# Seven products instead of eight for the experts' second product

## The chip, the cores and the metric

The kernel runs on one core of one Trainium2 chip. The metric is the device time of one execution in microseconds (us), as the median of the runs; the profile is of one further execution.

## The reference, cut to what matters

Attention (left out here) gives rows that a first MLP turns into `x`, 2304 tokens of 512 numbers. The part that the change touches is the last stage, eight experts that see every token; `P` is a 2304x8 table of weights, `F` is 1024:

```python
out = np.zeros((N, D), dtype=np.float32)
for e in range(E):                        # 8 experts
    h = np.maximum(x @ w1[e], 0.0)        # first product,  2304x512 @ 512x1024
    ye = h @ w2[e]                        # second product, 2304x1024 @ 1024x512
    out += P[:, e:e + 1] * ye
```

Everything is fp32. A number is held as a high and a low fp32r part, and one fp32 product is three matmuls: high by high, high by low, low by high (`mm3`, L79 to L82).

## The kernel before, in words

The expert stage starts some 655 us into the span and lasts to its end. It runs in *units* (L952 on). An expert's 1024 hidden columns are cut in two *blocks* (`NJ`), each of 256 columns from the lower and 256 from the upper half of `F` (`BF`), so there are 16 blocks. The 18 tiles of 128 tokens form three groups of six (`NUN`, `UP`), and a unit is one block for one group: 48 units.

In a unit, `hidden` (L882) makes the first product by Strassen's scheme in the variant with shared sums: seven products of halves in place of eight, in the order t1, b11, b22, t2, b21, t3, t4 of the operands made of x. Each product is done for two column tiles q = 0, 1 of 128 hidden columns: six matmuls that stream 384 tokens. A q step is called an *H step* here: 14 per unit, 84 matmuls of 128x384. The sums and differences of x are made once, kept in DRAM (`xs`), and loaded again for every unit through the ring `xr` of `XR` = 6 buffers (L737). The sums of w1 are made on POOL by `w1_prep` (L700) into the ring `w1o`. Products that are used more than once stay in PSUM and are accumulated on, or copied by ACT to a tile `u` (`kept`) and added by DVE (`plus`, L892). ReLU and the split into high and low parts is `relu_halves` (L875): ACT writes the high part (L877), DVE the low one (L878).

The second product is plain. Behind every second H step of a unit, `outputs` (L926) does one of the six token tiles of the unit before: four hidden tiles `h` by four tiles `w2o`, 12 matmuls of 128x512 into one PSUM bank `ps_acc`. That is called an *O step*, six per unit, 72 matmuls. DVE then scales the bank by a column of `pm` (that is `P`) and adds it to `acc` in SBUF (L944); in the first expert, where `pm` is not there yet, ACT copies (L938) or DVE adds (L940), and from the second expert on `acc` is scaled once on POOL (L943). The tiles `w2o` are made by `w2_prep` (L728): POOL writes the high part (`hi_pool`, L70) and the low part (`lo_pool`, L76) of each of four raw tiles of 128x512.

Each engine works through its instructions in one order, which a scheduler has fixed when the kernel is built; only waits on other engines move them. All loads go through one queue of SP, also in order: the loads of `xr`, and those of w1 and w2 (`w_load`, L680) into the ring `raw2`. A load whose buffer is not free holds back all loads behind it.

Of the kernel before, what the change touches and what calls it, by code (L numbers as in the profile page):

```python
# [21 lines left out]
def tile_kernel(ctx: ExitStack, tc, q, k, v, w_phi, w_in, w_out, w_gate, w1, w2, out):  # L22
# [37 lines left out]
    def bank(tag):  # L60
        return psp.tile([P, 512], F32, tag=tag, name="ps_" + tag, bufs=PS_BUFS[tag])
# [4 lines left out]
    def hi_act(dst, src, scale=1.0):  # L66
        nc.scalar.activation(dst, src, AF.Copy, scale=scale)
# [631 lines left out]


    def w1_prep(b):
        (a11, a12), (a21, a22) = (tuple(raw.pop((b, False, r, k)) for k in range(2)) for r in range(2))

        def add(x, y, op):
            t = wp.tile([P, 2, BF], F32, tag="ws", name="ws", bufs=3)
            nc.gpsimd.tensor_tensor(out=t, in0=x, in1=y, op=op)
            return t
# [12 lines left out]
        keep("s2", s2)  # L720
        yield
        keep("a12", a12)
        yield
        keep("s3", add(a11, a21, ALU.subtract))
        yield
        keep("a22", a22)
        yield

    def w2_prep(b):
        for i in range(2 * QB):  # L730
            w2t[b, i] = halves("w2o", 6, raw.pop((b, True) + divmod(i, QB)))
            yield

    def take(g, n):
        for _ in range(n):
            next(g, 0)
# [2 lines left out]
    WITH = {"t1": "s1", "b11": "a11", "b22": "s4", "t2": "s2", "b21": "a12", "t3": "s3", "t4": "a22"}  # L739
    units = [(b, c) for b in range(len(blocks)) for c in range(NUN)]  # L740
    wanted = [(c, o) for _, c in units for o in XOPS]
    XR = 6
    xring = []

    def x_ahead(n):
# [117 lines left out]
            )  # L863
            yield

    UB, HB = 8, 10

    side_work = []

# [5 lines left out]
    def relu_halves(src):  # L875
        t = hp_.tile([P, 2, UW], F32R, tag="h", name="h", bufs=HB)
        nc.scalar.activation(t[:, 0], src, AF.Relu)  # L877
        nc.vector.scalar_tensor_tensor(out=t[:, 1], in0=src, scalar=0.0, in1=f32(t[:, 0]), op0=ALU.max, op1=ALU.subtract)  # L878
        return t

    def hidden(b, c, n0, got):
        T, A, X = {}, {}, {}

        def kept(name, q, ps):
            T[name, q] = t = hp_.tile([P, UW], F32, tag="u", name="u", bufs=UB)
            nc.scalar.copy(t, ps)  # L888

        def plus(name, q, ps):  # L890
            t = T.pop((name, q))
            nc.vector.tensor_tensor(out=t, in0=ps, in1=t, op=ALU.add)  # L892
            return t

        for i, o in enumerate(XOPS):
            x_ahead(n0 + i + XR)
            x = xring[n0 + i]
            for q in range(QB):
                if o in ("t1", "b21"):
                    X[q] = bank("att")[:, 0:UW]  # L900
                if o == "b11":
                    A[q] = bank(("h", "kv")[q])[:, 0:UW]
                ps = (X if o in ("t1", "b22", "b21") else A)[q]
                product(ps, wops[b, WITH[o]], x, q, o in ("t1", "b11", "b21"))
                if b == 0 and q == 0:
                    for kh, t in {"t1": [(0, 1)], "b11": [(0, 0), (0, 1)], "b22": [(1, 1)], "b21": [(1, 0)]}.get(o, ()):
                        gate_add(x, kh, t)
                if o == "t1":
                    kept("p5", q, ps)
                elif o == "b11":  # L910
                    kept("p1", q, ps)
                elif o == "b22":
                    kept("p53", q, ps)
                elif o == "t2":
# [12 lines left out]

    def outputs(b, ti, hs, t):
        _, acc, pm = out_pool
        e, j = blocks[b]  # L930
        ps = bank("acc")
        ts_ = slice(t * P, (t + 1) * P)
        for i, h in enumerate(hs):
            w = w2t[b, i]
            mm3(ps, h[:, 0, ts_], h[:, 1, ts_], w[:, 0], w[:, 1], i == 0, i == 2 * QB - 1)
        a = acc[:, ti, :]
        if b == 0:
            nc.scalar.copy(a, ps)  # L938
# [12 lines left out]
    n0 = 0
    for b, c in units:  # L952
        got = {}
        for i, _ in enumerate(hidden(b, c, n0, got)):
            if not out_pool:
                with tc.high_priority(offset=-100):
                    make(2)
            if i % QB == QB - 1 and behind:
                outputs(*behind.pop(0))
        if not out_pool:  # L960
            make(99)
            ectx.close()
            mo = ctx.enter_context(tc.tile_pool(name="mo", bufs=1, reuse_waits="tile"))
            out_pool += [mo, mo.tile([P, NTT, DM], F32, name="acc"), mo.tile([P, NTT, E], F32, name="pm")]
            take(w2_prep(0), 9)
        n0 += len(XOPS)
        if b == 0:
            side_work.append(gate_end(c))
            next(side_work[-1])
            if c == NUN - 1:  # L970
                side_work.append(sinkhorn())
        behind = [
            (b, 2 * (UP * c + i) + t, [got["%d%d" % (r, t + 1), q] for r in (1, 2) for q in range(QB)], i)
            for t in (1, 0) for i in range(UP)
        ]
# [44 lines left out]
```

## Time and profile before

| | |
|---|---|
| median of 3 runs (lowest, highest) | 2190.03 us (2187.73, 2192.64) |
| the profiled execution's own time | 2189.35 us |
| its span | 2187.4 us |
| PE (matmul) busy | 2158.2 us, 99% |
| DVE, ACT, POOL busy | 48%, 32%, 23% |
| granted TensorE clock, mean of the span | 0.998 |

The profiled execution is 0.68 us under the median, and its span is 1.95 us shorter than its own time. A busy PE says only that matmuls follow each other without a gap; how close they follow is read from the starts of consecutive rows.

### The profile page before, as it was taken

How to read it: one execution, taken by the hardware profiler on the slowest of the kernel's cores; microseconds unless marked ns; L12 is line 12 of the kernel's file. 1: busy time of each engine (PE TensorE's matmuls, PEld its weight loads, DVE VectorE, ACT ScalarE, POOL GpSimd, SP SyncE). 2: the span in 40 equal slices, each digit the busy share in tenths (PEclk: the TensorE clock that was granted, in tenths of full speed). 3: DMA queues.
4: the chain of work that ended last, by engine and by line, in shares of the span. 5: the costliest groups of instructions: out<-in, count | busy, mean ns of one | idle time of the engine just before them, and what ended most of it. 6: DMA issues, size and time to landing. Idle time of an engine off the chain costs nothing.

```text
span 2187.4 us, 28996 instructions
## 1 busy us (share of the span) xinstructions
PE 2158.2 (99%) x11047; PEld 1903.2 (87%) x11047; DVE 1054.0 (48%) x1753; ACT 707.1 (32%) x1445; POOL 509.9 (23%) x537
## 2 busy tenths in 40 slices
PE   8999999999999999999999999999999999999999
PEld 6787888888888889998999899989998999899987
DVE  6998765754325264344334433443344334433443
ACT  6766655653223322222222222222222222222221
POOL 1001211100304133423313143131423313143100
PEclk9999999999999999999999999999999999999999
DMA  7798665647628555655555565655655556555553
GB/s 209 263 294 274 191 199 161 206 144 242 240 87 273 208 188 184 218 189 203 201 193 206 183 212 182 218 201 184 214 191 203 200 193 210 183 213 179 206 191 99
DMA packets 208699, 439.55 MB, mean 201 GB/s; under 512 B 74009, under 2 KB 130969, under 8 KB 208561
## 3 DMA queue, kind: packets, MB, share of 16 engines
q1 hardware_dynamic: 207280, 437.37, 59.3%
q8 instruction: 88, 1.44, 0.3%
q10 hardware_dynamic: 1280, 0.33, 0.1%
q14 instruction: 51, 0.41, 0.1%
HBM read 399.51 MB, written 38.12 MB: 200 GB/s over the span
## 4 chain that ended last, share of the span: by engine, by line
PE 93%; DVE 2%; ACT 2%; DMA 2%; SPq 1%; issue 1%; ACTq 0%; DVEq 0%
PE ps_acc L81 15%; PE ps_acc L82 15%; PE ps_acc L80 14%; PE ps_att L80 6%; PE ps_att L81 6%; PE ps_att L82 6%; PE ps_h L80 6%; PE ps_h L82 6%; PE ps_h L81 6%; PE ps_kv L82 4%; PE ps_kv L80 4%; PE ps_kv L81 4%; PE ps_att L86 1%; PE ps_kv L86 1%; DMA xs_t<-xo 1%
## 5 line engine op out<-in xcount | busy, mean ns | idle before, releaser
L944 DVE SCALAR_TENSOR_TENSOR acc<-ps_acc,pm,acc 128x512 f32<-128x512 f32 x252 | 189.1, 750 | 624.1 <-PE ps_acc L82 615.8
L82 PE MATMUL ps_acc<-w2o,h 128*128 128x512 f32 x1152 | 454.6, 395 | 0.0
L81 PE MATMUL ps_acc<-w2o,h 128*128 128x512 f32 x1152 | 453.9, 394 | 0.0
L80 PE MATMUL ps_acc<-w2o,h 128*128 128x512 f32 x1152 | 449.1, 390 | 0.3 <-ACT lt L855 0.3
L877 ACT ACTIVATE h<-u 128x384 fp32r<-128x384 f32 x288 | 140.6, 520 | 592.0 <-DVE u L892 592.0
L82 PEld LDWEIGHTS ps_acc<-w2o,h 128*128 128x128 f32 x1152 | 216.4, 188 | 45.9
L80 PEld LDWEIGHTS ps_acc<-w2o,h 128*128 128x128 f32 x1152 | 217.0, 188 | 39.8 <-ACT lt L855 0.7
L81 PEld LDWEIGHTS ps_acc<-w2o,h 128*128 128x128 f32 x1152 | 216.5, 188 | 39.9
L70 POOL TENSOR_SCALAR w2o<-raw 128x512 fp32r<-128x512 f32 x64 | 47.0, 735 | 649.4 <-PE ps_acc L82 557.4
L878 DVE SCALAR_TENSOR_TENSOR h<-u,h 128x384 fp32r<-128x384 f32 x288 | 190.6, 690 | 11.7
L80 PE MATMUL ps_att<-xr,w1o 128*128 128x384 f32 x576 | 194.0, 337 | 0.0
L82 PE MATMUL ps_att<-xr,w1o 128*128 128x384 f32 x576 | 193.8, 336 | 0.0
L81 PE MATMUL ps_att<-xr,w1o 128*128 128x384 f32 x576 | 193.3, 336 | 0.0
L888 ACT COPY u<-ps_att 128x384 f32<-128x384 f32 x192 | 92.1, 480 | 228.1 <-PE ps_att L82 228.1
L80 PE MATMUL ps_h<-xr,w1o 128*128 128x384 f32 x384 | 131.3, 342 | 0.0
L82 PE MATMUL ps_h<-xr,w1o 128*128 128x384 f32 x384 | 130.8, 341 | 0.0
L81 PE MATMUL ps_h<-xr,w1o 128*128 128x384 f32 x384 | 129.7, 338 | 0.0
L82 PE MATMUL ps_kv<-xr,w1o 128*128 128x384 f32 x384 | 128.4, 334 | 0.0
L80 PE MATMUL ps_kv<-xr,w1o 128*128 128x384 f32 x384 | 128.3, 334 | 0.0
L81 PE MATMUL ps_kv<-xr,w1o 128*128 128x384 f32 x384 | 128.3, 334 | 0.0
L70 POOL TENSOR_SCALAR w1o<-ws 128x512 fp32r<-128x512 f32 x64 | 40.7, 636 | 309.2 <-PE ps_att L82 307.8
L80 PEld LDWEIGHTS ps_att<-xr,w1o 128*128 128x128 f32 x576 | 108.2, 188 | 4.3 <-DVE xf L545 0.3
(250 smaller groups left out, 4074.3 us busy)
## 6 DMA issues: line engine op xcount, KB each, us to landing
xr<-xs_t SPq DMA_DIRECT2D x192, 768.0 KB
xr<-xs_b SPq DMA_DIRECT2D x144, 768.0 KB
w<-scratch SPq DMA_DIRECT2D x128, 512.0 KB
raw<-in_moe_w_dram SPq DMA_DIRECT2D x128, 256.0 KB
scratch<-cw SPq DMA_DIRECT2D x32, 512.0 KB
xs_t<-xo SPq DMA_DIRECT2D x36, 256.0 KB
raw<-in_moe_w_in_dram SPq DMA_DIRECT2D x16, 512.0 KB
raw<-in_moe_w_out_dram SPq DMA_DIRECT2D x16, 512.0 KB
```

What stands on the lines that cost most here:

```text
L70: nc.gpsimd.tensor_scalar(dst, src, 1.0, 1.0, op0=ALU.mult, op1=ALU.mult)
L80: nc.tensor.matmul(o, lhsT=wh, rhs=xh, start=start, stop=False, skip_group_check=chk)
L81: nc.tensor.matmul(o, lhsT=wh, rhs=xl, start=False, stop=False, skip_group_check=chk)
L82: nc.tensor.matmul(o, lhsT=wl, rhs=xh, start=False, stop=stop, skip_group_check=chk)
L86: nc.tensor.matmul(o, lhsT=w[0], rhs=x[0], start=start, stop=stop, skip_group_check=chk)
L877: nc.scalar.activation(t[:, 0], src, AF.Relu)
L878: nc.vector.scalar_tensor_tensor(out=t[:, 1], in0=src, scalar=0.0, in1=f32(t[:, 0]), op0=ALU.max, op1=ALU.subtract)
L888: nc.scalar.copy(t, ps)
L944: nc.vector.scalar_tensor_tensor(out=a, in0=ps, scalar=pm[:, ti, e:e + 1], in1=a, op0=ALU.mult, op1=ALU.add)
```

## The change

From the second expert on (block 2 of 16), the second product is done by the same scheme of seven products instead of eight half products. The first expert's two blocks stay as they were.

- `inner` (new) makes seven operands of the hidden tiles for each q: three (`a11`, `a22`, `a12`) are ReLU results, four (s1 to s4) are sums or differences of such, new operations of DVE. Five of the seven are split by `split`: ACT writes the high part, POOL the low part; `a22` and `a12` go through `relu_halves`.
- `w2_prep` makes seven split tiles of w2 for a block (three loaded quarters and four sums) instead of four; the four sums are new on POOL.
- `seconds` (new) does seven products, each for three pairs of token tiles and two q: 21 *S steps* of six matmuls of 128x256 per unit. Products accumulate on top of each other in chains in four fixed PSUM banks, and DVE reads the running sum after each product, scales it and adds it to a quarter of `acc` (L1059): 21 readings of 128x256 per unit.
- A unit's S steps run beside the H steps of the next unit, one behind each even and two behind each odd H step.
- Rings: `xr` 6 to 5, `raw2` 5 to 4, `w1o` 10 to 8, `w2o` 6 to 8, `u` 8 to 10, `h` 10 to 14. The w2 loads come in 128x2x256 pieces, and the preparation is called at other places.

```diff
+    WSB, W2B = 3, 8
...
-                t = wp.tile([P, 2 * BF], F32, tag="raw2", name="raw2", bufs=5)
+                t = wp.tile([P, 2 * BF], F32, tag="raw2", name="raw2", bufs=4)
...
+                if second and e:
+                    t = t.rearrange("p (q d) -> p q d", q=QB)
+                    nc.sync.dma_start(t, w2[e, f0:f0 + BF, k * HK:(k + 1) * HK].rearrange("(q p) d -> p q d", p=P))
...
+    def combine(x, y, op):
+        t = wp.tile([P, 2, BF], F32, tag="ws", name="ws", bufs=WSB)
+        nc.gpsimd.tensor_tensor(out=t, in0=x, in1=y, op=op)
+        return t
...
-            wops[b, o] = halves("w1o", 10, src)
+            wops[b, o] = halves("w1o", 8, src)
...
+        (b11, b12), (b21, b22) = (tuple(raw.pop((b, True, r, k)) for k in range(2)) for r in range(2))
+        keep("b11", b11)
+        yield
+        t1 = combine(b12, b11, ALU.subtract)
+        keep("t1", t1)
+        yield
+        t2 = combine(b22, t1, ALU.subtract)
+        keep("t2", t2)
+        yield
+        keep("t3", combine(b12, b22, ALU.subtract))
+        yield
+        keep("b22", b22)
+        yield
+        keep("t4", combine(b21, t2, ALU.subtract))
+        yield
+        keep("b21", b21)
+        yield
...
-    XR = 6
+    XR = 5
...
-    UB, HB = 8, 10
+    UB, HB = 10, 14
...
+    def split(t, src):
+        hi_act(t[:, 0], src)
+        lo_pool(t[:, 1], src, t[:, 0])
+        return t
...
+    def inner(b, o, q, T, got, ps, plus):
+        if o == "t2":
+            T["r21", q] = t = plus("p53", q, ps)
+            nc.scalar.activation(t, t, AF.Relu)
+        elif o == "b21":
+            T["r11", q] = t = plus("p1", q, ps)
+            nc.scalar.activation(t, t, AF.Relu)
+            got["a11", q] = split(new_h(), t)
+            s3 = new_u()
+            nc.vector.tensor_tensor(out=s3, in0=T["r21", q], in1=t, op=ALU.subtract)
+            got["s3", q] = split(new_h(), s3)
+        elif o == "t3":
+            t = plus("p5", q, ps)
+            s1 = T.pop(("r21", q))
+            nc.vector.scalar_tensor_tensor(out=s1, in0=t, scalar=0.0, in1=s1, op0=ALU.max, op1=ALU.add)
+            got["s1", q] = split(new_h(), s1)
+            s2 = T["s2", q] = T.pop(("r11", q))
+            nc.vector.tensor_tensor(out=s2, in0=s1, in1=s2, op=ALU.subtract)
+            got["s2", q] = split(new_h(), s2)
+            got["a22", q] = relu_halves(t)
+        elif o == "t4":
+            got["a12", q] = relu_halves(ps)
+            s4 = new_u()
+            nc.vector.scalar_tensor_tensor(
+                out=s4, in0=ps, scalar=0.0, in1=T.pop(("s2", q)), op0=ALU.max, op1=ALU.subtract
+            )
+            got["s4", q] = split(new_h(), s4)
...
+    SECOND = (
+        ("a11", "b11", "a", 0, 0), ("s1", "t1", "x", 1, 1), ("s2", "t2", "a", 0, 1), ("s3", "t3", "a", 1, 1),
+        ("s4", "b22", "x", 0, 1), ("a22", "t4", "a", 1, 0), ("a12", "b21", "y", 0, 0),
+    )
...
+    def seconds(b, c, got):
...
+        at_ = {
+            "a": [(b0, 0, 1), (b0, 1, 0), (b1, 0, 1)],
+            "x": [(b2, 0, 1), (b2, 1, 0), (b1, 1, 0)],
+            "y": [(b3, 0, 1), (b3, 1, 0), (b2, 0, 1)],
+        }
...
+                for q in range(QB):
+                    h = got[ho, q][:, :, i * P:(i + 1) * P]
+                    mm3(ps, h[:, 0], h[:, 1], w[:, 0, q], w[:, 1, q], first and q == 0, True, True)
+                due.append((i, ps))
+                if i == 0:
+                    yield
+                    continue
+                for i_, ps in due:
...
+                    nc.vector.scalar_tensor_tensor(
+                        out=a, in0=ps, scalar=pm[:, ti, e:e + 1], in1=a, op0=ALU.mult, op1=ALU.add
+                    )
...
+            if pending:
+                take(pending, 1 + odd)
+            elif odd and behind:
                 outputs(*behind.pop(0))
+            if odd and c == NUN - 1 and b + 1 < len(blocks):
+                take(coming, 1)
+            if odd and c == 0 and b:
+                take(late, 1)
...
-            take(coming, (1, 3, 9)[c])
-            if c == 1:
+            take(coming, (0, 1, 9)[c])
+            if c == NUN - 1:
                 w_load(b + 1, True)
-            take(late, (0, 0, 2)[c])
-    for x in behind:
-        outputs(*x)
+                late = w2_prep(b + 1)
+    for _ in pending:
+        pass
```

On DVE, this is the part of a unit from its product t3 on, in the kernel before (`ps_h` and `ps_kv` are the banks of q = 0 and 1, L892 is `plus`, L878 the low part, L944 the reading):

```order
L892 TENSOR_TENSOR u_14012<-ps_h_14039,u_14012 128x384
L892 TENSOR_TENSOR u_14021<-ps_kv_14048,u_14021 128x384
L878 SCALAR_TENSOR_TENSOR h_14180<-u_14012,h_14180 128x384
L878 SCALAR_TENSOR_TENSOR h_14190<-u_14021,h_14190 128x384
L878 SCALAR_TENSOR_TENSOR h_14193<-u_14046,h_14193 128x384
L878 SCALAR_TENSOR_TENSOR h_14196<-u_14055,h_14196 128x384
L944 SCALAR_TENSOR_TENSOR acc_7297<-ps_acc_14199,pm_7298,acc_7297 128x512
L878 SCALAR_TENSOR_TENSOR h_14221<-ps_h_14039,h_14221 128x384
```

The same part on DVE with the change (L959 is now `plus`, L936 and L939 make s1 and s2, L906 is the low part, L1059 the reading, L945 makes s4):

```order
L959 TENSOR_TENSOR u_12936<-ps_h_12973,u_12936 128x384
L936 SCALAR_TENSOR_TENSOR u_13025<-u_12936,u_13025 128x384
L939 TENSOR_TENSOR u_12980<-u_13025,u_12980 128x384
L959 TENSOR_TENSOR u_12951<-ps_kv_12988,u_12951 128x384
L936 SCALAR_TENSOR_TENSOR u_13039<-u_12951,u_13039 128x384
L906 SCALAR_TENSOR_TENSOR h_13182<-u_12936,h_13182 128x384
L939 TENSOR_TENSOR u_12995<-u_13039,u_12995 128x384
L1059 SCALAR_TENSOR_TENSOR acc_7295<-ps_acc_9060,pm_7296,acc_7295 128x256 x2
L1059 SCALAR_TENSOR_TENSOR acc_7295<-ps_acc_9061,pm_7296,acc_7295 128x256
L906 SCALAR_TENSOR_TENSOR h_13206<-u_12951,h_13206 128x384
L906 SCALAR_TENSOR_TENSOR h_13237<-ps_h_12973,h_13237 128x384
L945 SCALAR_TENSOR_TENSOR u_13240<-ps_h_12973,u_12980 128x384
```

Five operations with two inputs in SBUF (L936, L939, L906 from `u`) now stand ahead of the readings of banks 9060 and 9061, which the next unit's first product writes again.

On POOL, this is a stretch of the preparation in the kernel before, where a block's last w2 tiles are split and the next block's w1 sums begin (L706 makes a sum `ws`; `raw2` are loaded quarters):

```order
L70 TENSOR_SCALAR w2o_17224<-raw2_16742 128x512
L76 TENSOR_TENSOR w2o_17224<-raw2_16742,w2o_17224 128x512
L706 TENSOR_TENSOR ws_17235<-raw2_17231,raw2_17233 128x512
L70 TENSOR_SCALAR w1o_17237<-ws_17235 128x512
L70 TENSOR_SCALAR w1o_17470<-raw2_17227 128x512
L76 TENSOR_TENSOR w1o_17237<-ws_17235,w1o_17237 128x512
L76 TENSOR_TENSOR w1o_17470<-raw2_17227,w1o_17470 128x512
L706 TENSOR_TENSOR ws_17473<-ws_17235,raw2_17227 128x512
L70 TENSOR_SCALAR w2o_17732<-raw2_17483 128x512
```

The same place on POOL with the change, at the end of the first unit of a block (L707 makes the sums; `h` are low parts of the hidden operands, the last four of the ten of a unit among them):

```order
L70 TENSOR_SCALAR w2o_13280<-raw2_12923 128x512
L76 TENSOR_TENSOR h_13199<-u_13039,h_13199 128x384
L76 TENSOR_TENSOR w2o_13280<-raw2_12923,w2o_13280 128x512
L76 TENSOR_TENSOR h_13203<-u_12995,h_13203 128x384
L707 TENSOR_TENSOR ws_13618<-raw2_13287,raw2_13289 128x512
L76 TENSOR_TENSOR h_13242<-u_13240,h_13242 128x384
L70 TENSOR_SCALAR w1o_13620<-ws_13618 128x512
L707 TENSOR_TENSOR ws_13708<-ws_13618,raw2_13283 128x512
L76 TENSOR_TENSOR w1o_13620<-ws_13618,w1o_13620 128x512
L707 TENSOR_TENSOR ws_13710<-raw2_13285,ws_13708 128x512
L707 TENSOR_TENSOR ws_13856<-raw2_13283,raw2_13287 128x512
L76 TENSOR_TENSOR h_13262<-u_13260,h_13262 128x384
```

The hidden operands' low parts now queue among the weights' preparation: `h_13262`, the last s4, stands behind four sums that wait for the load of `raw2_13289`.

On SP's queue, the loads around the same place before (`xs_1_b21` is product b21's operand for the second token group):

```order
L749 DMA xr_14171<-xs_1_t2_130 128x1536
L749 DMA xr_14213<-xs_1_b21_131 128x1536
L691 DMA raw2_14245<-in_moe2_w1_dram 128x2x256
L688 DMA raw2_14495<-in_moe2_w2_dram 128x512
L749 DMA xr_14252<-xs_1_t3_132 128x1536
```

And with the change:

```order
L777 DMA xr_13229<-xs_1_t2_130 128x1536
L695 DMA raw2_13289<-in_moe2_w1_dram 128x2x256
L777 DMA xr_13291<-xs_1_b21_131 128x1536
L689 DMA raw2_13974<-in_moe2_w2_dram 128x2x256
L777 DMA xr_13332<-xs_1_t3_132 128x1536
```

The load of `raw2_13974` takes the buffer of `raw2_13287`, which POOL's last sum above reads, and the operand of t3 for the second unit stands right behind it.

## Rows read from the trace of the kernel before

**Rows 1.** The page, part 1: busy time, share and instructions of each engine

```profile
PE 2158.2 (99%) x11047; PEld 1903.2 (87%) x11047; DVE 1054.0 (48%) x1753; ACT 707.1 (32%) x1445; POOL 509.9 (23%) x537
```

**Rows 2.** Stretches of one unit each: busy of PE, PEld, DVE, ACT, POOL; clock; DMA

```profile
1500.97:1532.25 31.28, 31.28 (x158) 28.23 (x157) 11.95 (x20) 6.79 (x14) 0.00 (x0) 1.00 0.51 176
1532.25:1563.53 31.28, 31.28 (x158) 28.23 (x157) 13.45 (x20) 6.80 (x14) 18.91 (x18) 1.00 0.63 230
1563.53:1594.81 31.28, 31.28 (x158) 28.23 (x157) 12.83 (x20) 6.79 (x14) 7.84 (x8) 1.00 0.56 193
```

**Rows 3.** Timeline of DVE, readings of acc: start, length, instruction, idle before

```profile
1533.53 0.75 DVE L944 SCALAR_TENSOR_TENSOR acc<-ps_acc,pm,acc 128x512 f32<-128x512 f32 x1 [2.21 <-PE ps_acc L82]
...
1559.94 0.75 DVE L944 SCALAR_TENSOR_TENSOR acc<-ps_acc,pm,acc 128x512 f32<-128x512 f32 x1 [0.99 <-PE ps_acc L82]
...
1564.81 0.75 DVE L944 SCALAR_TENSOR_TENSOR acc<-ps_acc,pm,acc 128x512 f32<-128x512 f32 x1 [2.20 <-PE ps_acc L82]
```

**Rows 4.** Timeline of PE: first matmul of 12 H, of 12 O, and after

```profile
1509.02 0.33 PE L80 MATMUL ps_att<-xr,w1o 128*128 128x384 f32 x1
...
1511.10 0.39 PE L80 MATMUL ps_acc<-w2o,h 128*128 128x512 f32 x1
...
1513.86 0.33 PE L80 MATMUL ps_h<-xr,w1o 128*128 128x384 f32 x1
```

**Rows 5.** Timeline of PE and PEld, first MLP: 12 matmuls of 128x256, and after

```profile
641.95 0.28 PE L80 MATMUL ps_att<-gh,w 128*128 128x256 f32 x1
641.95 0.19 PEld L81 LDWEIGHTS ps_att<-gl,w 128*128 128x128 f32 x1
642.06 0.28 PE L81 MATMUL ps_att<-gl,w 128*128 128x256 f32 x1
...
643.38 0.40 PE L80 MATMUL ps_h<-xhi,w 128*128 128x512 f32 x1
```

**Rows 6.** Groups of DVE by shape: count, then busy us, mean ns, idle before

```profile
L892 DVE TENSOR_TENSOR u<-ps_h,u 128x384 f32<-128x384 f32 x96 | 53.5, 558 | 50.3 <-PE ps_h L82 50.3
...
L509 DVE SCALAR_TENSOR_TENSOR u<-t,ps_kv 128x256 f32<-128x256 f32 x16 | 6.7, 421 | 7.5 <-ACT t L507 7.5
```

**Rows 7.** Tile h, low parts from SBUF: shortest, median and longest, ns

```profile
L878 DVE SCALAR_TENSOR_TENSOR h<-u,h x288: 545/553/1642, 668.9 to 2163.3; 128x384 fp32r<-128x384 f32 x144
```

**Rows 8.** Timeline of DVE, two sets of four low parts

```profile
1504.83 2.17 DVE L878 SCALAR_TENSOR_TENSOR h<-u,h 128x384 fp32r<-128x384 f32 x4
...
1536.11 3.88 DVE L878 SCALAR_TENSOR_TENSOR h<-u,h 128x384 fp32r<-128x384 f32 x4
```

**Rows 9.** Timeline of POOL beside the second of these sets

```profile
1536.38 0.75 POOL L70 TENSOR_SCALAR w2o<-raw 128x512 fp32r<-128x512 f32 x1 [39.52 <-PE ps_acc L82]
1537.22 1.47 POOL L76 TENSOR_TENSOR w2o<-raw,w2o 128x512 fp32r<-128x512 f32 x1
```

**Rows 10.** Groups of ACT and POOL by shape

```profile
L877 ACT ACTIVATE h<-u 128x384 fp32r<-128x384 f32 x288 | 140.6, 520 | 592.0 <-DVE u L892 592.0
...
L76 POOL TENSOR_TENSOR w1o<-ws,w1o 128x512 fp32r<-128x512 f32 x64 | 82.6, 1291 | 2.5
...
L70 POOL TENSOR_SCALAR w1o<-ws 128x512 fp32r<-128x512 f32 x64 | 40.7, 636 | 309.2 <-PE ps_att L82 307.8
...
L76 POOL TENSOR_TENSOR vl<-vr,vh 128x320 fp32r<-128x320 f32 x16 | 14.9, 951 | 0.2
...
L76 POOL TENSOR_TENSOR wpl<-wpr,wph 128x256 fp32r<-128x256 f32 x1 | 0.7, 724 | 0.0
```

**Rows 11.** Timeline of SP and POOL: a load, and the sum that waits for it

```profile
1538.71 0.38 SPq L691 DMA_DIRECT2D raw<-in_moe_w_dram  x1
...
1541.47 1.29 POOL L706 TENSOR_TENSOR ws<-raw,raw 128x512 f32<-128x512 f32 x1 [0.33 <-DMA raw<-in_moe_w_dram]
```

**Rows 12.** The page, part 6: issues of the two kinds of load

```profile
xr<-xs_t SPq DMA_DIRECT2D x192, 768.0 KB
...
raw<-in_moe_w_dram SPq DMA_DIRECT2D x128, 256.0 KB
```

More of the change, by code (lines that the diff above doesn't have):

```diff
@@ L698, in halves @@
         return t
+    def combine(x, y, op):
+        t = wp.tile([P, 2, BF], F32, tag="ws", name="ws", bufs=WSB)
+        nc.gpsimd.tensor_tensor(out=t, in0=x, in1=y, op=op)
+        return t
     def w1_prep(b):
         (a11, a12), (a21, a22) = (tuple(raw.pop((b, False, r, k)) for k in range(2)) for r in range(2))
[L704 to L707, printed above, removed]
+        add = combine
         def keep(o, src):
-            wops[b, o] = halves("w1o", 10, src)
+            wops[b, o] = halves("w1o", 8, src)
         s1 = add(a21, a22, ALU.add)
@@ L729, in w2_prep, with keep @@
     def w2_prep(b):
-        for i in range(2 * QB):
-            w2t[b, i] = halves("w2o", 6, raw.pop((b, True) + divmod(i, QB)))
-            yield
+        def keep(o, src):
+            w2t[b, o] = halves("w2o", W2B, src)
+        if blocks[b][0] == 0:
+            for i in range(2 * QB):
+                keep(i, raw.pop((b, True) + divmod(i, QB)))
+                yield
+            return
+        (b11, b12), (b21, b22) = (tuple(raw.pop((b, True, r, k)) for k in range(2)) for r in range(2))
[15 more added lines that the diff above has]
+        yield
     def take(g, n):
@@ L879, in relu_halves, with new_h, new_u @@
         return t
+    def split(t, src):
+        hi_act(t[:, 0], src)
+        lo_pool(t[:, 1], src, t[:, 0])
+        return t
+    def new_h():
+        return hp_.tile([P, 2, UW], F32R, tag="h", name="h", bufs=HB)
+    def new_u():
+        return hp_.tile([P, UW], F32, tag="u", name="u", bufs=UB)
+    def inner(b, o, q, T, got, ps, plus):
[25 more added lines that the diff above has]
+            got["s4", q] = split(new_h(), s4)
     def hidden(b, c, n0, got):
@@ L913, in hidden @@
                     kept("p53", q, ps)
+                elif b >= NJ:
+                    inner(b, o, q, T, got, ps, plus)
                 elif o == "t2":
@@ L948, in outputs @@
             side_work.pop(0)
+    SECOND = (
+        ("a11", "b11", "a", 0, 0), ("s1", "t1", "x", 1, 1), ("s2", "t2", "a", 0, 1), ("s3", "t3", "a", 1, 1),
+        ("s4", "b22", "x", 0, 1), ("a22", "t4", "a", 1, 0), ("a12", "b21", "y", 0, 0),
+    )
+    banks = []
+    def seconds(b, c, got):
+        _, acc, pm = out_pool
+        e, j = blocks[b]
+        if not banks:
+            banks.extend(bank("acc") for _ in range(4))
+        b0, b1, b2, b3 = banks
+        at_ = {
[3 more added lines that the diff above has]
+        }
+        seen, scaled = set(), set()
+        for ho, wo, ch, t, n in SECOND:
+            w = w2t[b, wo]
+            due = []
+            for i in range(UP):
+                pb, half, first = at_[ch][i]
+                first = bool(first) and ch not in seen
+                ps = pb[:, half * HK:(half + 1) * HK]
+                for q in range(QB):
[3 more added lines that the diff above has]
+                if i == 0:
+                    yield
+                    continue
+                for i_, ps in due:
+                    ti = 2 * (UP * c + i_) + t
+                    if b == NJ and ti not in scaled:
+                        scaled.add(ti)
+                        nc.gpsimd.tensor_scalar(
+                            acc[:, ti, :], acc[:, ti, :], pm[:, ti, 0:1], 1.0, op0=ALU.mult, op1=ALU.mult
+                        )
+                    a = acc[:, ti, n * HK:(n + 1) * HK]
+                    nc.vector.scalar_tensor_tensor(
+                        out=a, in0=ps, scalar=pm[:, ti, e:e + 1], in1=a, op0=ALU.mult, op1=ALU.add
+                    )
+                    if b == len(blocks) - 1 and wo in ("b21", "t4"):
+                        store(ti)
+                due = []
+                yield
+            seen.add(ch)
     behind = []
+    pending = None
     n0 = 0
@@ L957, in tile_kernel @@
                     make(2)
-            if i % QB == QB - 1 and behind:
+            odd = i % QB
+            if pending:
+                take(pending, 1 + odd)
+            elif odd and behind:
                 outputs(*behind.pop(0))
+            if odd and c == NUN - 1 and b + 1 < len(blocks):
+                take(coming, 1)
+            if odd and c == 0 and b:
+                take(late, 1)
         if not out_pool:
@@ L971, in tile_kernel @@
                 side_work.append(sinkhorn())
[L972 to L975, printed above, removed]
+        if b >= NJ:
+            pending = seconds(b, c, got)
+        else:
+            behind = [
+                (b, 2 * (UP * c + i) + t, [got["%d%d" % (r, t + 1), q] for r in (1, 2) for q in range(QB)], i)
+                for t in (1, 0) for i in range(UP)
+            ]
         if c == 0:
```

4 lines of the change are left out of this document (2 added, 2 removed).

## The prediction, made before the changed kernel was run

> **What bounds the kernel now.** I read the page's shares first: PE is busy 99% of the span, no other engine over 48% [rows 1]. A busy PE can still be a waiting one, so the second view is the table of stretches. One unit is 31.28 us, the distance of the same reading in two units (1533.53 and 1564.81) [rows 3]; in three such stretches PE is busy for all 31.28, at the full clock (1.00, the 2.4 GHz level), DVE for 12 to 13.5, ACT for 6.8, POOL for 0 to 18.9 [rows 2]. The third view says what fills them. PE's timeline has 12 H matmuls from 1509.02 to 1511.10, 2.08 us, and 12 O matmuls from there to 1513.86, 2.76 us [rows 4]. Readings a pair of H steps and one O step apart lie 4.87 us apart (1559.94, 1564.81) [rows 3]: 2.08 + 2.76 + 0.03, so a switch from one kind to the other costs about 0.03. Seven H pairs, six O steps and six switches make 14.56 + 16.56 + 0.18 = 31.30, the unit as measured. Only fewer or shorter matmul slots shorten it.
>
> **Matmuls removed and added.** 42 units (14 blocks of three) change. Each loses 72 O matmuls, 16.56 us, and gets 126 of 128x256. The first MLP has just such a run, each with a weight load of its own: 12 from 641.95 to 643.38, 1.43 us or 0.119 each [rows 5]. So 126 x 0.119 = 15.02, a gain of 1.54 per unit and of 64.9 in 42. That the columns fall by an eighth (32256 for 36864) but the time only by 9% is the price of 54 more matmuls.
> The weight loads last 0.19 in the record, longer than the 0.119 slot, yet a load stands beside each matmul and the next starts on time [rows 5]: they are hidden.
> The Trainium skill ("TensorE: Matmul & The Clock Gate", The mechanism) says that a weight load overlaps matmuls in flight only when its row group differs; all loads here take the whole array, so by it every S slot would hold a load and a matmul. The trace disagrees, with 0.119 for both.
>
> **Switches.** H and S steps alternate 14 times a unit instead of six: eight more at 0.03 [rows 3] are 0.24, or 10 in all; the 256-wide run of the MLP shows none at its ends [rows 5]. Bounds 0 and 10; I take 5.
>
> **DVE.** Before, a unit has 20 operations. After it has six additions `plus` at 0.558 [rows 6], eight operations with two SBUF inputs (s1, s2, s3, the low part of a22, two q each), four on PSUM (low part of a12, s4) at 0.558, and 21 readings of 128x256; the nearest row of that width is 0.421 [rows 6]. The two-input price depends on POOL: four low parts take 2.17 with POOL idle, 0.54 each, and 3.88 while POOL works, 0.97 each [rows 8, 9]; the longest of all is 1.64 [rows 7]. Sum: 3.35 + 4.3 to 7.8 + 2.2 + 8.8 = 18.7 to 22.2 of 29.8. That fits, so throughput is no bound; the place to look at is the end of a unit. From the end of t3's first H step (five pairs of 4.25 and one H step into the unit, 22.3; 0.2 for the drain of the last matmul, whose record, 0.33, outlasts its slot) two `plus`, five two-input operations and two readings stand before PE may write the same bank in the next unit's second slot, at 29.8 + 1.05 = 30.8. At 0.97 they need 1.12 + 4.85 + 0.84 = 6.8 and end at 29.3: 1.5 us to spare. I price it at nothing; above 1.27 per operation PE waits.
>
> **ACT** gets 16 operations of 0.52 for six [rows 10], so 6.8 + 5.2 = 12.0 of 29.8 [rows 2]; DVE's slack above is also that of what it feeds.
>
> **POOL.** A block has 14 split tiles (0.64 + 1.29) and eight sums (1.29) [rows 10], 37.3, plus 30 low parts of 128x384. No row has that width; 256, 320 and 512 took 0.72, 0.95 and 1.29 [rows 10], so 0.95 to 1.29, and I take 1.0, near the line through them: 30. Together 67 of a block's 89, up to 76 at the upper bound, 27 before [rows 2]. The tight place is the end of a block's first unit. The split of t4's tile can start at 21.4, when PE has left its buffer; three tile halves, five low parts and b21's last half later (2.6 + 5.0 + 1.3) it is 30.3. Then SP may load `raw2_13289`; a load of its size landed 2.7 us after its issue (1538.71 to 1541.44) [rows 11], so the next sum starts at 33.0, and with it seven operations (four sums, one split, one low part: 5.2 + 1.9 + 1.0) end at 41.1. Only then does SP issue `raw2_13974` and behind it t3's operand for the next unit. That is 768 KB, the load ahead 256 [rows 12]; at 345 GB/s (193 GB/s at a share of 0.56 [rows 2]) the 768 KB beyond the first 256 take 2.3 more, and the issue ahead 0.4 [rows 11], so it is there at 41.1 + 0.4 + 2.7 + 2.3 = 46.5, and wanted at 29.8 + 21.2 = 51.0. The last low part of s4 is done at 42.1 and wanted at 29.8 + 17.0 + 1.05 = 47.9. So 4.5 and 5.8 us to spare. Interference stretches POOL too: its operations beside the contended set took 0.75 and 1.47 for 0.64 and 1.29 [rows 9], some 0.15 each, 2.5 on this chain. It still holds, priced at nothing. The smaller `xr` ring costs only lead: four pairs, 17 us.
>
> **Small waits.** All these margins are of 1.5 to 6 us and 21 readings release banks in each unit; PE will not be as gapless as before. Between nothing and 1 us per unit I take 0.2: 8.
>
> **Sum.** The profiled execution took 2189.35: minus 64.9, plus 5, plus 8, is 2137.5; the median was 0.7 above it: 2138.
>
> **The rivals.**
> *POOL's chain is late.* Where the walk above is over 4.5 us longer, t3's operand comes late once a block, in 14 blocks. At 1.29 per low part (1.7 more for six), 0.4 of interference on some 16 operations (6.4) it is 8.1 longer, 3.6 late: 2138 + 14 x 3.6 = 2188; halfway, 2163. For it: POOL goes from 29% to 75% busy [rows 2] and holds SP's queue; against it: a quarter of the block is still free.
> *DVE is late in every unit (slower).* With POOL in work nearly all the time, a two-input operation waits out a POOL operation and more. If the five ahead of the readings take the longest seen, 1.64 [rows 7], they end at 32.7, 1.9 late, 80 us in 42 units: 2218. It decides from 1.27; at 1.56 each, the gain of 61 us is used up. For it: 0.97 and 1.64 come from a kernel with POOL at 29%. Against it: POOL is idle for long in a block's second unit, and 0.97 already is a stretch of full work.
> The Trainium skill ("SBUF — State Buffer", Who interferes with whom) says that a DVE instruction with two SBUF inputs contends with a GpSimd instruction that reads SBUF, an exclusive lock for the whole instruction; the 0.54 against 0.97 agree with it.
> *Small waits everywhere.* Where 21 readings and smaller rings cost the 1 us per unit of the bound above: 2130 + 42 = 2172.
> *Loads are not hidden at 256 columns (slower).* Were the 54 more loads paid at their recorded 0.19, a unit would be 10.3 longer instead of 1.5 shorter, over 2560. Rows 5 speak against it.
>
> **How the numbers follow.** PE stays the bound with small waits: 0.64, 2125 to 2158, 2138 the likeliest. POOL late or small waits everywhere: 0.19, 2158 to 2192. DVE late: 0.15, above 2185. Loads: 0.02. The range leaves out the fast end below 2122 and most of the slow cases: 2122 to 2188. A measurement of this kernel can tell about 0.2% (4 us) from no change. Faster: 0.64, most of the second case and the edge of the third, 0.81; same 0.05; slower 0.14.
>
> **What would show it.** In a stretch of one unit: its length 29.8 to 30.2 instead of 31.28; 12 S matmuls in 1.43; PE waits on DVE under 0.5 a unit; readings near 0.42; low parts of 384 on POOL near 1.0; two-input operations of DVE under 1.27 on average. Wrong it is if units come out over 31, and then PE's waits name the case: on DVE at the banks `ps_acc` early in a unit, on the load `xr` of t3 in a block's second unit, or none at all and slots longer than 0.119.

## The result, and the profile after

The changed kernel took 2133.73 us (median of 4 runs, 2127.82 to 2135.14), the kernel before 2191.33 beside it (4 runs, 2187.73 to 2192.64): a ratio of 0.9735, 95% interval 0.9712 to 0.9757. The forecast was 2138. The profiled execution is the fastest of the four, 2127.82 with a span of 2126.0. Its span is 61.4 us shorter than that of the profile before (2187.4), 3.8 more than the medians show.

Where the time went is read in five steps. The first is the page's part 1, after:

```profile
PE 2089.0 (98%) x13315; PEld 1956.8 (92%) x13315; DVE 1424.6 (67%) x2551; ACT 905.6 (43%) x1865; POOL 1134.7 (53%) x1097
```

Against [rows 1], PE has 2268 instructions more and 69 us less; it is still the bound. DVE, ACT and POOL together have some 1200 us more work.

Second, three stretches of 29.82 us of the kernel after, which answer to [rows 2] (columns as there):

```profile
1500.00:1529.82 29.82, 29.82 (x214) 29.75 (x214) 21.83 (x39) 11.48 (x24) 24.37 (x22) 1.00 0.51 191
1529.82:1559.64 29.82, 29.82 (x215) 29.82 (x214) 21.56 (x41) 11.72 (x25) 20.39 (x20) 1.00 0.65 226
1559.64:1589.46 29.82, 29.49 (x209) 29.20 (x208) 21.70 (x40) 11.40 (x25) 26.70 (x26) 1.00 0.60 212
```

The length of a stretch comes from an operation that occurs once a unit, s4 of q = 0. This is its group in the view of the tile `u`: count, shortest, median and longest in ns, first and last start:

```profile
L945 DVE SCALAR_TENSOR_TENSOR u<-ps_h,u x42: 537/541/543, 880.4 to 2103.1; 128x384 f32<-128x384 f32 x42
```

(2103.1 − 880.4) / 41 = 29.82 a unit, for 31.28 before. The three stretches give POOL 71.5 us of a block's 89.5, DVE 21.7 and ACT 11.5 a unit. In the third PE lacks 0.33.

Third, PE's timeline, the first slots of a unit:

```profile
1505.26 0.34 PE L80 MATMUL ps_att<-xr,w1o 128*128 128x384 f32 x1
...
1507.04 0.34 PE L80 MATMUL ps_att<-xr,w1o 128*128 128x384 f32 x1
...
1508.09 0.28 PE L80 MATMUL ps_acc<-w2o,h 128*128 128x256 f32 x1
...
1509.51 0.34 PE L80 MATMUL ps_h<-xr,w1o 128*128 128x384 f32 x1
...
1534.87 0.34 PE L80 MATMUL ps_att<-xr,w1o 128*128 128x384 f32 x1
```

An H step takes 1.05 (1507.04 to 1508.09), the 12 S matmuls behind it 1.42, this pair 4.25 (1505.26 to 1509.51), this unit 29.61, so a pair 4.23 on average. The next unit, up to the H step at 1564.46 below, takes 29.59. The prediction's slots alone, 14.56 and 15.02, make 29.58: a change of kind costs nothing that can be seen here. Before, it cost 0.03 [rows 3], and one row more of that trace shows where:

```profile
1515.97 0.39 PE L80 MATMUL ps_acc<-w2o,h 128*128 128x512 f32 x1
```

The H pair at 1509.02 in [rows 4], a unit's first, follows another H pair and takes 2.08. The pair at 1513.86 follows an O step and takes 2.11, up to this row. The starts in [rows 4] span both changes of kind and add up to 4.84, so the 0.03 lies inside the pair behind an O step.

Fourth, PE's waits over the whole span (us, times, longest), the largest group:

```profile
PE ps_acc L80 <- DVE acc L1059: 6.7, 17, 1.1
```

Of the 17, 14 stand at one place per block, the first S step of a block's first unit (4.8 us); three, 1.9 us with the longest, come after the last H step. PE's timeline at that place:

```profile
1564.46 0.34 PE L80 MATMUL ps_att<-xr,w1o 128*128 128x384 f32 x1
...
1566.00 0.36 PE L80 MATMUL ps_acc<-w2o,h 128*128 128x256 f32 x1 [0.33 <-DVE acc L1059]
...
1594.64 0.34 PE L80 MATMUL ps_att<-xr,w1o 128*128 128x384 f32 x1
```

The H step that begins at 1564.46 should hand over at 1565.51; the S step starts at 1566.00, 0.49 late, and this unit is 30.18 long. What it waited for is in DVE's timeline:

```profile
1558.07 1.26 DVE L936 SCALAR_TENSOR_TENSOR u<-u 128x384 f32<-128x384 f32 x1
1559.43 1.47 DVE L939 TENSOR_TENSOR u<-u 128x384 f32<-128x384 f32 x1
1560.83 0.54 DVE L959 TENSOR_TENSOR u<-ps_kv,u 128x384 f32<-128x384 f32 x1
1561.41 0.80 DVE L936 SCALAR_TENSOR_TENSOR u<-u 128x384 f32<-128x384 f32 x1
1562.13 1.65 DVE L906 SCALAR_TENSOR_TENSOR h<-u,h 128x384 fp32r<-128x384 f32 x1
1563.70 1.37 DVE L939 TENSOR_TENSOR u<-u 128x384 f32<-128x384 f32 x1
1564.99 1.26 DVE L1059 SCALAR_TENSOR_TENSOR acc<-ps_acc,pm,acc 128x256 f32<-128x256 f32 x3
```

and in POOL's beside it:

```profile
1558.88 1.61 POOL L707 TENSOR_TENSOR ws<-raw,ws 128x512 f32<-128x512 f32 x1
1560.45 1.34 POOL L76 TENSOR_TENSOR h<-u,h 128x384 fp32r<-128x384 f32 x1
1561.76 1.61 POOL L707 TENSOR_TENSOR ws<-raw,raw 128x512 f32<-128x512 f32 x1
1563.32 1.34 POOL L76 TENSOR_TENSOR h<-u,h 128x384 fp32r<-128x384 f32 x1
```

The five two-input operations ahead of the readings take 1.26 + 1.47 + 0.80 + 1.65 + 1.37 = 6.55, 1.31 each. POOL has no gap there, and its operations are stretched too: 1.61 for 1.30, 1.34 for 1.02. At the ends of the two units before, the same five took 5.59 (from 1499.27, also beside a POOL without gaps) and 5.26 (from 1528.89, POOL at work for three quarters of the time), 1.12 and 1.05 each, and the S step was not late.

Fifth, the end of the span: the first matmul behind the last H step, before and after, and PE's waits from there on in the kernel after:

```profile
2165.90 0.39 PE L80 MATMUL ps_acc<-w2o,h 128*128 128x512 f32 x1
```

```profile
2099.36 0.28 PE L80 MATMUL ps_acc<-w2o,h 128*128 128x256 f32 x1
PE ps_acc L80 <- DVE acc L1059: 1.9, 3, 1.1
```

From there to the end of the span it is 21.5 us before and 26.7 after, although the slots are as long: six O steps (16.56) have become the last two S steps of one unit and the 21 of the last (16.4 in all). These S steps have no H steps beside them. Up to the last matmul it is 3.0 us more, 1.9 of them in those waits, and behind it 2.2 more.

### The profile page after: what moved, and what is told of

It reads as the page before. It is cut to its first block, busy times and chain, and to the rows that moved or that the text cites. A ratio compares the mean times of both kernels' runs of the same rounds, so it can differ in the third digit from the quotient of the medians.

```text
span 2126.0 us, 35902 instructions
## 1 busy us (share of the span) xinstructions
PE 2089.0 (98%) x13315; PEld 1956.8 (92%) x13315; DVE 1424.6 (67%) x2551; ACT 905.6 (43%) x1865; POOL 1134.7 (53%) x1097
## 4 chain that ended last, share of the span: by engine, by line
PE 80%; DVE 9%; DMA 3%; issue 3%; ACT 2%; POOL 1%; SPq 1%; ACTq 0%; DVEq 0%; POOLq 0%
PE ps_acc L80 12%; PE ps_acc L82 12%; PE ps_acc L81 12%; PE ps_att L80 6%; PE ps_att L81 6%; PE ps_att L82 5%; PE ps_h L80 5%; PE ps_h L82 5%; PE ps_h L81 5%; PE ps_kv L81 3%; PE ps_kv L80 3%; PE ps_kv L82 3%; DVE u L939 2%; DVE acc L1059 2%; DVE u L936 1%
## 5 line engine op out<-in xcount | busy, mean ns | idle before, releaser
L80 PE MATMUL ps_acc<-w2o,h 128*128 128x256 f32 (+1 forms) x1908 | 552.8, 290 | 6.7 <-DVE acc L1059 6.7
L82 PE MATMUL ps_acc<-w2o,h 128*128 128x256 f32 (+1 forms) x1908 | 553.7, 290 | 0.0
L81 PE MATMUL ps_acc<-w2o,h 128*128 128x256 f32 (+1 forms) x1908 | 552.7, 290 | 0.0
L76 POOL TENSOR_TENSOR h<-u,h 128x384 fp32r<-128x384 f32 x420 | 465.0, 1125 | 159.6 <-ACT h L67 115.4
L1059 DVE SCALAR_TENSOR_TENSOR acc<-ps_acc,pm,acc 128x256 f32<-128x256 f32 x882 | 374.1, 473 | 212.1 <-PE ps_acc L82 208.1
L80 PEld LDWEIGHTS ps_acc<-w2o,h 128*128 128x128 f32 x1908 | 359.5, 188 | 17.4 <-ACT h L67 9.5
L67 ACT ACTIVATE h<-u 128x384 fp32r<-128x384 f32 x420 | 220.9, 526 | 344.4 <-DVE u L945 99.8
L82 PEld LDWEIGHTS ps_acc<-w2o,h 128*128 128x128 f32 x1908 | 360.9, 189 | 5.8
L81 PEld LDWEIGHTS ps_acc<-w2o,h 128*128 128x128 f32 x1908 | 360.4, 189 | 5.0
L707 POOL TENSOR_TENSOR ws<-raw,raw 128x512 f32<-128x512 f32 x60 | 82.6, 1377 | 136.7 <-DVE u L509 79.6
L70 POOL TENSOR_SCALAR E<-E 128x1024 fp32r<-128x1024 f32 (+1 forms) x24 | 22.4, 932 | 189.5 <-ACT E L305 107.9
L906 DVE SCALAR_TENSOR_TENSOR h<-u,h 128x384 fp32r<-128x384 f32 x120 | 122.0, 1025 | 1.1
```

Of the source, the lines that this page charges most:

```text
L70: nc.gpsimd.tensor_scalar(dst, src, 1.0, 1.0, op0=ALU.mult, op1=ALU.mult)
```

## The experiments

All ran beside the kernel before (2189.2 to 2190.5); ratios are to it. Units are measured as above.

**after_again: the changed kernel once more,** on the chip of actlow, early and threes.

> The changed kernel once more, as the measure for the others of this call. All theories: 2134 us, within 4. In its trace a block should again show one wait of PE on DVE of about 0.5 us, at the second slot of a block's first unit, and none elsewhere.

2134.28 (0.9742, 0.9728 to 0.9755), unit 29.82, PE's wait on DVE 6.7 us in 17 times again. Where this run differs from the first profile is ahead of the changed units: the first H step of all starts at 659.5 instead of 655.4, the first one with S steps beside it at 886.4 instead of 878.4, and the spans are 7.8 apart. So the spread between these two executions does not come from the changed units.

**actlow: POOL freed of the hidden operands' low parts.** ACT writes the high part a second time in their place; the subtraction is left out.

```diff
     def split(t, src):
         hi_act(t[:, 0], src)
-        lo_pool(t[:, 1], src, t[:, 0])
+        hi_act(t[:, 1], src)
```

> The ten low parts per unit that POOL makes for the hidden operands are written by ACT instead, as a second copy of the high part (the low part's subtraction is left out); POOL keeps only the weights. Theory (POOL's reads stretch DVE's operations with two SBUF inputs, and these cause the wait): the two-input operations fall from about 1.0 to 1.4 us to 0.55 to 0.8, the wait once a block is gone, 8 us less, about 2126. Rival (the operations are long by themselves, or ACT, from 12 to 17 us a unit, now becomes late): two-input operations over 1.0 still, or waits of PE on ACT, and 2134 or more.

2123.51 (0.9691, 0.9677 to 0.9705). No wait on DVE, POOL or ACT is left in the units; two stretches of it, columns as above:

```profile
1500.00:1529.50 29.50, 29.50 (x211) 29.50 (x211) 19.62 (x41) 15.43 (x36) 9.82 (x9) 1.00 0.58 207
1529.50:1559.00 29.50, 29.50 (x212) 29.50 (x211) 18.12 (x37) 14.10 (x32) 15.51 (x15) 1.00 0.58 199
```

PE is full. The stretches are 29.50 long after the mean distance of s4's starts, 29.51, which is short of a unit: the first two of the 42 starts lie only 26.6 apart. PE's own rows, the first matmul of two units, give 29.59, as in the third unit of a block with the change:

```profile
1502.76 0.34 PE L80 MATMUL ps_att<-xr,w1o 128*128 128x384 f32 x1
...
1532.35 0.34 PE L80 MATMUL ps_att<-xr,w1o 128*128 128x384 f32 x1
```

So 29.59 is what the slots need. And DVE's two-input operations got shorter, though nothing in them changed. Their groups (shortest, median, longest), first of the kernel after, then of this one:

```profile
L906 DVE SCALAR_TENSOR_TENSOR h<-u,h x120: 541/1022/1650, 668.1 to 2101.7; 128x384 fp32r<-128x384 f32 x120
L936 DVE SCALAR_TENSOR_TENSOR u<-u x84: 557/962/1362, 873.3 to 2097.0; 128x384 f32<-128x384 f32 x84
L939 DVE TENSOR_TENSOR u<-u x84: 557/1369/1471, 874.8 to 2099.2; 128x384 f32<-128x384 f32 x84
```

```profile
L906 DVE SCALAR_TENSOR_TENSOR h<-u,h x120: 539/555/1652, 669.2 to 2092.8; 128x384 fp32r<-128x384 f32 x120
L936 DVE SCALAR_TENSOR_TENSOR u<-u x84: 557/559/966, 876.3 to 2089.6; 128x384 f32<-128x384 f32 x84
L939 DVE TENSOR_TENSOR u<-u x84: 547/560/1544, 877.3 to 2090.5; 128x384 f32<-128x384 f32 x84
```

What POOL's low parts cost through the others is 11 us (2134.28 against 2123.51); by the units, (29.82 − 29.59) x 42 = 10.

**early: all readings earlier in DVE's order.**

```diff
+                    with tc.high_priority(offset=100):
                         nc.vector.scalar_tensor_tensor(
                             out=a, in0=ps, scalar=pm[:, ti, e:e + 1], in1=a, op0=ALU.mult, op1=ALU.add
                         )
```

> The readings of the sums get a higher priority, so that on DVE the three readings of a22's product stand ahead of s2 of q = 1 and of the low parts of a22, not behind. Theory (PE's only regular wait is the bank that those readings release, 0.5 to 0.6 us once in each of 14 blocks, because five two-input operations stand ahead of them): the wait goes and nothing else changes, 8 us less than the changed kernel, about 2126. Rival (DVE as a whole is late there, so the wait only moves to the next thing that DVE owes, a22's low part or the banks of the hidden products): 2134.

2157.31 (0.9848, 0.9834 to 0.9862), 23 us slower than the change. PE's largest wait, DVE's timeline, and the matmul that waits:

```profile
PE ps_h L80 <- DVE u L946: 18.9, 27, 1.8
```

```profile
1613.87 1.47 DVE L907 SCALAR_TENSOR_TENSOR h<-u,h 128x384 fp32r<-128x384 f32 x1 [1.07 <-ACT h L906]
1615.26 0.54 DVE L907 SCALAR_TENSOR_TENSOR h<-ps_h,h 128x384 fp32r<-128x384 f32 x1
1615.73 1.25 DVE L1061 SCALAR_TENSOR_TENSOR acc<-ps_acc,pm,acc 128x256 f32<-128x256 f32 x3
1616.90 0.54 DVE L946 SCALAR_TENSOR_TENSOR u<-ps_h,u 128x384 f32<-128x384 f32 x1
```

```profile
1617.50 0.44 PE L80 MATMUL ps_h<-xr,w1o 128*128 128x384 f32 x1 [0.97 <-DVE u L946]
```

Three readings now stand ahead of s4, which frees the bank `ps_h`, and DVE idles 1.07 with nothing to fill it. The stall of the S step is gone; a larger one stands at `ps_h`. Neither branch of the expectation had a loss.

**early2: only a22's readings earlier** (`offset=100 if ho == "a22" else 0` in the same place).

> Only the readings of a22's product are put forward on DVE; those of the last product y stay behind s4, whose operation releases the bank of the hidden product b11. The run with all readings forward was 23 us slower, with PE waiting 0.7 us in two of three units for s4 (L946), and its trace had DVE idle 1.07 us before the second low part of a22, which waits for ACT there. Theory (DVE's chain at a unit's end is tight, and its order decides which bank comes late; the slots of PE are the same): the wait for a22's readings goes, s4 is 0.9 us earlier than with all readings forward and comes just in time, a unit of 29.5 to 29.7 instead of 29.82, so 2122 to 2130. Rival (the idle gap before a22's second low part, now uncovered, makes s4 late in most units): units of 29.9 to 30.2, 2138 to 2150.

2133.09 (0.9739, 0.9726 to 0.9753), unit (2107.7 − 887.6) / 41 = 29.76. No wait of a block's first S step on DVE is left, but the unit still takes 29.98 (1510.81 to 1540.79), with smaller latenesses in place of that wait. No difference from the change that can be measured: less than the theory expected, and not the rival's loss.

**threes: three S steps behind each odd H step.**

```diff
-                take(pending, 1 + odd)
+                take(pending, 3 * odd)
```

> S steps run in threes behind each odd H step: 7 changes between H and S in each direction fewer... that is half the switches of a unit. By the prediction's price of 0.03 us per switch 7 fewer would give 9 us over 42 units. By the trace of the changed kernel (H steps of 1.04 to 1.05 and S steps of 0.71 whatever stands ahead of them) switches cost nothing: slots the same, 14 x 1.045 + 21 x 0.711 = 29.6 per unit. In both cases the first S step starts one H step later, so the wait on DVE of 0.5 us once a block should go too: 8 us. So 2126 if switches are free, 2117 if they cost 0.03; 2134 or more if three steps in a row bring waits on the banks.

2132.15 (0.9732, 0.9719 to 0.9746), unit 29.73; 18 S matmuls take 2.15, the rate of the twelve above. Half the switches gain nothing: a unit without lateness takes 29.64 (1507.08 to 1536.72), for 29.59 with all of them. The stall of the S step is gone here too, but a block's first unit still takes 29.97, its lateness now at `ps_h` and `ps_kv`. So the 8 us that the expectation gave for the stall did not come.

**combo: early2 and threes together.**

> Three S steps behind each odd H step, together with a22's readings of y handed out earlier (the two edits that each took the stall of a block's first S step away). If the stall is what is left beside the shared lock of DVE and POOL: 2130 to 2132, units of 29.65 to 29.7. If each edit only moves the lateness to the next bank that DVE owes: as either alone, 2132 to 2134.

2134.02 (0.9745, 0.973 to 0.976), unit 29.83. The second branch held: PE now waits for `ps_kv`, which s4 of q = 1 frees.

**hiact2: high parts of all weight tiles on ACT.**

```diff
     def halves(tag, bufs, src):
-        hi_pool(t[:, 0], src)
+        hi_act(t[:, 0], src)
```

> The high parts of the 14 weight tiles of a block are written by ACT instead of POOL (10 us of POOL's 73 per block; ACT gets 3 us more per unit on 12). Nothing is left out. Theory (what makes DVE late is how much POOL reads beside it; without POOL's ten low parts a unit took 29.51, PE's bare slots): some of the 13 us between 29.82 and 29.51 come back, units of 29.6 to 29.75, 2124 to 2131. Rival (ACT works in order, and a weight tile that waits for POOL's sum or for a buffer now holds up the hidden operands behind it): waits of PE on ACT or on weights, 2140 or more.

2164.85 (0.989, 0.9876 to 0.9903), 31 slower than the change. Its ACT timeline, and PE's wait:

```profile
1539.78 0.63 ACT L67 ACTIVATE w2o<-raw 128x512 fp32r<-128x512 f32 x1 [6.92 <-DMA raw<-in_moe_w_dram]
1540.32 0.46 ACT L955 COPY u<-ps_h 128x384 f32<-128x384 f32 x1
```

```profile
1540.83 0.45 PE L80 MATMUL ps_h<-xr,w1o 128*128 128x384 f32 x1 [2.28 <-ACT u L955]
```

The rival held. ACT waits 6.92 us for a w2 load, and the copy that frees `ps_h` stands behind. (The 29.51 of the expectation is the mean by s4; PE's rows give 29.59.) Less work on POOL, but a weight's wait has been put onto an engine that releases banks.

**poolmore: the low parts of q = 0 written twice on POOL.**

```diff
-        lo_pool(t[:, 1], src, t[:, 0])
+        for _ in range(n):              # n = 2 for q = 0, 1 for q = 1
+            lo_pool(t[:, 1], src, t[:, 0])
```

> The five low parts of a unit for q = 0 are written twice on POOL. In the changed kernel POOL is busy 73 us of a block's 89.4 (24.4 a unit) and the end of its chain leaves about 2.2 us of margin once a block, before t3's operand xr is late. Five more operations of 1.1 us add 5.6 a unit, so POOL would need 30.0 of a 29.8 us unit. Theory (POOL's chain is the next bound, the margin is small): PE waits on the load xr and on h or w2o, units of 30.5 or more, 2165 or slower (+31 or more). Rival (POOL has slack that the scheduler's order can use): under +10.

2216.45 (1.0124, 1.0109 to 1.0139): 83 slower than the change, and slower than before. Its unit is (2190.9 − 885.5) / 41 = 31.84; a stretch, and PE's largest waits:

```profile
1500.00:1531.84 31.84, 29.77 (x208) 29.07 (x207) 21.33 (x39) 11.28 (x24) 30.12 (x29) 1.00 0.44 158
```

```profile
PE ps_acc L82 <- POOL h L76: 26.2, 26, 1.3
PE ps_kv L80 <- DVE u L960: 21.7, 13, 3.9
```

POOL, busy for 30.1 of 31.84, is the bound. No wait on `xr` appears, as the expectation had it beside `h`: late low parts come first.

**xr4: the ring `xr` with 4 buffers** (`XR = 4`).

> The ring xr with 4 buffers instead of 5. In the order of SP's queue b21's operand for a block's second unit then also stands behind the load of w1's last quarter. Theory (the ring is lead, and the lead that is left at the end of a block's first unit is some 2 us): one pair of steps, 4.25 us, less lead makes an operand about 2 us late once a block, 14 blocks: 2162 (+28), with PE waiting on the load xr. Rival (lead is plentiful): 0 to +4, no wait.

2162.26 (0.9877, 0.9858 to 0.9896). The end of POOL's last sum of a block's first unit, SP's queue, PE's wait there and in all:

```profile
1536.00 1.29 POOL L707 TENSOR_TENSOR ws<-raw,raw 128x512 f32<-128x512 f32 x1
```

```profile
1537.31 0.38 SPq L689 DMA_DIRECT2D raw<-in_moe_w_dram  x1
1537.79 0.42 SPq L777 DMA_DIRECT2D xr<-xs_b  x1
```

```profile
1542.45 0.41 PE L80 MATMUL ps_att<-xr,w1o 128*128 128x384 f32 x1 [1.78 <-DMA xr<-xs_b]
```

```profile
PE ps_att L80 <- DMA xr<-xs_b: 22.1, 13, 2.1
```

The sum ends at 1537.29, SP issues the load that waited for it and then b21's operand; PE has it 5.14 us after the first issue (0.4 + 2.7 + 2.3 = 5.4 in the prediction's walk). One buffer less costs 28 us (2162.26 against 2134.28), some 2 in each of the 13 blocks in which PE waits for the load; after the last block there is none to load for.

**half: the scheme from the fifth expert on,** 24 units instead of 42 (the conditions on the second expert moved to the fifth).

> The scheme of seven products starts at the fifth expert instead of the second: 24 units of 42 changed, all ring sizes as in the changed kernel. Theory (each changed unit gains 31.28 - 29.82 = 1.46 us of PE time, and nothing else matters): 24 x 1.46 = 35, so 2190.5 - 35 = 2155. Rival (part of the gain comes from the rings and the other places of the preparation, in all units): under 2150. Rival (the change between the two forms, or the last unit without H steps beside it, costs something once): 2155 plus that, over 2160.

2159.13 (0.9863, 0.9849 to 0.9876): 30.1 us for 24 units; the change has 56.2 for 42 (after_again). At 1.46 a unit they should be 35.0 and 61.3: both are 5 short. The 18 units between the two bring 26.1, 1.45 each. So the gain goes with the units, less some 5 us once, as the last branch of the expectation had it; it is of the size of the longer end above.

**rings: the kernel before with the new ring sizes alone.**

```diff
-    XR = 6
+    XR = 5
-    UB, HB = 8, 10
+    UB, HB = 10, 14
```

(and `raw2` 5 to 4, `w1o` 10 to 8, `w2o` 6 to 8.)

> The kernel before with the new sizes of the six rings alone (xr 5, raw2 4, w1o 8, w2o 8, u 10, h 14), the second product as it was. Theory (PE never waited for a ring before, and four pairs of lead cover the loads): 2190, within 4. Rival (the smaller xr ring, or raw2 with POOL behind it, holds PE up even at POOL's old load): over 2196. Rival (larger u and h rings alone bring part of the gain): under 2184.

2189.83 against 2189.24 (0.9996, 0.9987 to 1.0005): nothing.

## Why the prediction was right

The mechanism held: PE stayed the bound, its slots got shorter by somewhat more than the working's amount, and the waits stayed small. By the forecast's steps:

- **Matmuls, right.** A pair takes 4.23 on average, 12 S matmuls 1.42, as worked out. 54 more weight loads a unit are hidden. (The rival for them has a slip: units 10.3 longer would give over 2620; 2560 goes with 10.3 − 1.5.)
- **Switches, mis-sized, with the wrong sign.** Forecast was +5 in all, on top of six of 0.03 a unit that before already had. The slots alone take 29.59, so they gave (31.28 − 29.59) x 42 = 71 us, where the forecast had 64.9 − 5 = 59.9: the old 0.18 a unit has gone and nothing has come. In threes, half the switches cost no less.
- **Small waits, right in size, wrong in shape.** Forecast 0.2 a unit, 8 in all; (29.82 − 29.59) x 42 = 10. Not spread over 21 readings: some 0.58 of each block (30.18 against 29.60 for its other units), 8 us in 14 blocks, stands at one S step.
- **The end, put at nothing.** The prediction counts 42 units alike. The last one's S steps have no H steps beside them, and from the last H step on the kernel takes 5 us longer than before; 1.9 of it are PE's waits on DVE, and what makes the rest was not tried. 71 − 10 − 5 = 56 agrees with the medians (57.6 and, in after_again, 56.2), for 51.9 forecast. That the forecast came this near is in part luck: the slots gave 11 us more than it had, and waits and end took back 7 of them.
- **DVE, right, and nearer the edge than priced.** The threshold of 1.27 per operation held: at 1.31 PE waits, at 1.12 and 1.05 it does not. The readings cost 0.473 instead of 0.42, and one of the five operations took 1.65, as much as the slow case feared for all. The slower rival was the right mechanism, with its condition met in one unit of three. The kernels show the cause: with POOL's low parts gone, medians of 0.96 to 1.37 fall to 0.56 and the stall goes.
  The Trainium skill ("SBUF — State Buffer", Who interferes with whom) has the pair of ports that DVE and GpSimd share as an exclusive lock. Both engines being stretched (1.37 for 0.56, 1.34 for 1.02) agrees with it.
- **POOL, right in the sum; the chain had less to spare.** 71.5 us a block in the stretches, for 67 to 76. A low part of 384 took 1.02 in the median but 1.13 on average, for 1.0. The last sum ended at 1518.99, 13.7 into the block's second unit (1505.26), for 41.1 − 29.8 = 11.3 in the walk, so the operand of t3 was some 2.1 early, not 4.5 (worked out; its landing is not in the rows). xr4 shows that this lead is real: with one buffer less, PE waits. poolmore shows how near POOL is: 5.2 us more a unit (1353.4 busy in all for 1134.7) and it is the bound.
- **Loads, right.** Landing after 2.7 us (issue 1508.38, sum at 1511.11) is as in [rows 11]. POOL's timeline, this sum and the last of its chain, and SP's issue of the load that the first waits for:

```profile
1511.11 1.30 POOL L707 TENSOR_TENSOR ws<-raw,raw 128x512 f32<-128x512 f32 x1 [1.78 <-DMA raw<-in_moe_w_dram]
...
1517.67 1.32 POOL L707 TENSOR_TENSOR ws<-raw,raw 128x512 f32<-128x512 f32 x1
```

```profile
1508.38 0.38 SPq L695 DMA_DIRECT2D raw<-in_moe_w_dram  x1
```

What stays open: a version with neither the stall nor POOL's share in DVE's time. Of the runs that do the whole computation, threes, early2 and combo are within the spread of the change (2132.15 to 2134.02), none better by what can be measured. Why an H pair behind an O step took 0.03 more before, and behind S steps takes no more now, was not tried.

## What to carry to other kernels

Price a DVE operation with two SBUF inputs at what it takes beside a busy POOL (here 0.96 to 1.37 in the median for 0.56), and count how many stand ahead of the operation that frees a bank: that, not the engine's share, says when PE waits. Handing the readings out earlier only moves the lateness to the next bank; put the edit where the order has slack, and take what is late next into account. A ring that costs nothing at one size (`xr` at 5: nothing in the kernel before, no wait on it with the change) can cost 28 us one buffer lower, since a load stands in one queue with loads that wait for another engine. Steps that run beside the next unit have nothing beside them in the last one: price that end by itself (here 5 us).

## What was not expected of the hardware

- PE changes between 384-column and 256-column matmuls at no cost that can be seen (29.59 a unit for 29.58 of slots). Beside 512-column matmuls an H pair took 2.11 for 2.08, and not at the changes but inside the pair.
- Interference of POOL and DVE is mutual: POOL's sums of 128x512 took 1.61 for 1.30, its low parts 1.34 for 1.02, beside DVE operations of up to 1.65 for 0.55.
- A reading of 128x256 (PSUM, a column of `pm`, and `acc`) took 0.473, where another operation of that width on a PSUM bank took 0.421 [rows 6].
